# Bias and scores of two batches by 64x64 blocks of the matrix engine in an attention, Fourier and feed-forward kernel

## The chip, the core and the metric

The kernel runs on one core of a Trainium2 chip. A core has five engines with instruction streams of their own, which meet only through semaphores: the matrix engine (TensorE, PE in the profile; its weight loads are PEld), the vector engine (VectorE, DVE), the scalar engine (ScalarE, ACT), GpSimd (POOL) and SyncE (SP), which here issues most of the DMAs. PE reads SBUF and writes PSUM; ACT and DVE bring results back. The metric is the device time of one execution in microseconds.

## The reference

Four batches, 8 heads, 768 positions, 64 numbers per head. Attention with 8 global keys and a local window of 96, with a bias that falls linearly with distance; its output, 768 x 512 per batch, goes through a real-valued two-dimensional Fourier transform, a residual, a normalisation and a feed-forward layer of 512 to 2048 to 512.

```python
scores = scale * np.matmul(q, k.transpose(0, 1, 3, 2))
rel = pos[:, None] - pos[None, :]
keep = (pos[None, :] < n_global) | ((rel >= 0) & (rel < n_local))
dist = np.where(is_global & ~is_local, float(n_local), np.abs(rel))
bias = -slopes[:, None, None] * dist[None, :, :]
scores = np.where(keep, scores + bias[None], -1e9)
a = softmax(scores)
x = np.matmul(a, v)                       # (batch, 768, 512) after the heads are joined
u = x + np.real(np.fft.fft(np.fft.fft(x, axis=1), axis=2))
un = (u - mean(u)) / np.sqrt(var(u) + 1e-6)
out = u + np.maximum(un @ w_ch1, 0.0) @ w_ch2
```

## The kernel before

**Units and stages.** A unit is one pair of heads of one batch: n = 4 b + hp, 16 in all. For each unit q and k are loaded as float32 (`load`, L350), cast to half precision (`cast_qk` L405, `cast_direct` L423; the profile's tile `qk`), and transposed so that the 64 numbers of a head lie on partitions (`trans`, L556: 12 transposes on PE into `pt`, evacuated into `qkT` by DVE at L574 or ACT at L578; in batches 2 and 3 by DMA, `trans_dma`). In `qkT` the first head of the pair lies on partitions 0 to 63, the second on 64 to 127.

**Scores.** `score` (L585) works on one unit in three groups g = 0, 1, 2, each with two tiles of 128 keys against up to 256 queries (496, 480 and 384 columns per head in all). A group has a PSUM pair of banks `sc`, one bank for each head s. In batches 0 and 1 (`pem`) PE adds the bias too: for each head it multiplies a 128x128 diagonal matrix `sid`, holding minus 8 times the head's slope, with the table of distances `dist` (L600, L605), and then adds the scores, whose 64-row operands for the two heads stand in the upper and lower half of the array (L616). ACT takes the exponential straight into `ex` (L639). In batches 2 and 3 PE makes the scores alone (L614), ACT takes their exponential into `er`, and DVE multiplies by `mk` (L651), the exponential of the biased distances, which ACT makes once from `dist` (L1371, queued behind batch 1's attention).

**After the scores.** `v` is cast by POOL (L444) and, in batches 0 and 1, put in place by PE (`v_place`, 64x64 blocks of the identity, L460, tile `pvp`; evacuated by DVE L478 and ACT L479). The global keys go apart: POOL picks them out of `qkT` into `kG` (L532), then `glob` and `v_global`. `av` (L724) multiplies and DVE normalises (L769, L770) into `x`. The batch is written to DRAM and read back in another row order (`bounce`: L789 writes `xd`, L797 reads `xr`). Then the transform: DVE folds (`fold_s`, `fold_d`, L817 to L928), PE makes `py` (L954), its mirror is copied by POOL (L1002), PE makes `pu` (L1034), DVE adds the residual (L1053, L1062), and the normalised `un` is transposed: `nt_unit`, on PE into `ptu` (L1123, evacuated by ACT L1131 or DVE L1133) for pairs c below 7, by a DMA transpose from SP (`nt_dma`, L1108) for the later ones. The feed-forward layer follows for 12 pairs of rows c: `ph` (L1151, eight groups of 16 matmuls per pair), the relu of ACT or DVE (L1157, L1158), `pg` (L1175), the last sum on DVE (L1184) and the store (L1189). For pairs from 8 on a variant takes the place of `pg` (L1256 and around).

**Buffers.** The two weight matrices (loaded by POOL, L1407 and L1412, in eight blocks) lie where q and k of batch 1 were staged, so their load stands behind the last cast of q and k of unit 7. The first loads of batch 2 stand behind the last weight block (`hold`, L1421). `hT` has three buffers; one of them holds `x` of batch 1 first. `sc`, `pt`, `pvp`, `pav`, `py` and `pu` share four pairs of PSUM banks until the first `ph`, two pairs after that, and `ph` and `pg` have two banks each.

**The order.** All of it is issued in an order that a planner makes while the kernel is built (`Plan`): it keeps a clock for each engine and DMA stream, takes PE's work from four lists (mix, attention, `ph`, `pg`) and everything else from a list of pending pieces with the durations written in the code, and always issues the piece that can start first; `rank` breaks ties. A piece of rank below 0 is taken as if it were 0.8 us earlier (`AHEAD`); `RF` gives this rank to the fold of batch 0. The durations in the code have a part in the order only.

Of the kernel before, what the change touches and what calls it, by code (L numbers as in the profile page):

```python
# [9 lines left out]
FP16 = mybir.dt.float16  # L10
# [12 lines left out]
class Plan:  # L23
# [62 lines left out]
    def first(self):  # L86

        best = None
        for i, (ready, p) in enumerate(self.ready):
            if p[11]:  # L90
                ready = [max(r, self.lanes[p[11] - 1]) for r in ready]
            c = (min(max(self.t[w[0]], r) for w, r in zip(p[1], ready)) - self.AHEAD * (p[10] < 0), p[10], ready[0], p[0], i)
            if best is None or c < best:
                best = c
        return best
# [44 lines left out]
    LOOK = 10  # L140
    AHEAD = 0.8

    def run(self, streams):

        left = [list(s) for s, _ in streams]
        while True:
            best = None
            for i, s in enumerate(left):
                for k, (needs, ring, _) in enumerate(s[:self.LOOK if streams[i][1] else 1]):
                    if not self.known(needs):  # L150
                        continue
                    r = self.at(needs, "PE")
                    if ring is not None:

                        there = [(min(self.rings[g])[0], g) for g in ring
                                 if self.rings[g] and not (g in ("C", "D") and ("CD",) in self.tok)]
                        if not there:
                            continue
                        t, g = min(there)
                        r = max(r, t + self.SEM)  # L160
                    else:
                        g = None
                    c = (max(r, self.t["PE"]), i, k, g or "")
                    if best is None or c < best:
                        best = c
# [3 lines left out]
            elif best is not None:  # L169
                needs, ring, fn = left[best[1]].pop(best[2])  # L170
                fn(best[0], self.slot(best[3]) if ring is not None else "")
                self.promote()
# [28 lines left out]
def kernel(  # L201
# [40 lines left out]
    dist = np.concatenate([np.where(band, rel, np.where(kk < NG, NL, far)), near, near[:, 0:P]], 1)  # L242
    NM = 256 + 256 + P
    pp = np.arange(P)[:, None]
    mm = np.arange(P)[None, :]
# [73 lines left out]
    idn = ident[:, 0:128]  # L319
    dist_sb = kon.tile([P, NM], FP16, tag="dist", name="dist")  # L320
    sid = kon.tile([P, H, P], FP16, tag="sid", name="sid")
# [28 lines left out]
    def load(b, hp, which):  # L350
# [3 lines left out]
        if b >= FB:  # L354
            srcs = [(0, q), (1, k)] if which == "qk" else [(2, v)]
            for w, src in srcs:
                i = 1 + HP + 3 * (n - FB * HP) + w

                def run(src=src, i=i, w=w):
# [5 lines left out]
                    for t2 in range(2):  # L365
                        nc.sync.dma_start(t[64 * t2:64 * t2 + 64], x[t2])
                pl.later([("SP", 0.55 if w < 2 else 1.1, run)], free("qs", i) + gate, 0.0, [("ld", n, w)], lat=1.7, dma=1.65 if w < 2 else 2.7, nd=1 + (w > 1))
                if w < 2:
# [79 lines left out]
    def v_place(b, hp):  # L448
        n = HP * b + hp

        def run(start, ring):
# [11 lines left out]
            if n == 0:  # L463
                idle(14)
            e = pl.pe(mm_us(P, 12), start)
            pl.used(("free", "v0", n), e)
# [71 lines left out]
    def trans_dma(b, hp):  # L538
# [11 lines left out]
        for x, (w, a) in enumerate(((0, 0), (1, 0), (1, 1))):  # L550
            pl.later([("SP", 1.3, lambda w=w, a=a: xb(w, a))], [("qk", n, w)] + (free("qkT", n) if x == 0 else [("xb", n, x - 1)]), 0.0,
                     [("xb", n, x)], lat=1.7, dma=1.35 if x == 0 else 0.7)
        pl.later([("SP", 0.0, lambda: None)], [("xb", n, x) for x in range(3)], 0.0, [("qkT", n)], [("free", "qk", n)])
# [31 lines left out]
    def score(b, hp, g):  # L585
# [3 lines left out]
        def run(start, ring):  # L589
# [6 lines left out]
            if pem:  # L596
                for s in range(2):
                    lhsT = sid[:, 2 * hp + s, :]
                    if g == 1:
                        nc.tensor.matmul(pa[:, s, :].rearrange("p (i c) -> p i c", i=2)[:, :, 0:CO], lhsT,  # L600
                                         dist_sb[:, 256:256 + CO].unsqueeze(1).to_broadcast([P, 2, CO]),
                                         start=True, stop=False, skip_group_check=True)
                    else:
                        m0 = (0, 0, 256)[g]
                        nc.tensor.matmul(pa[:, s, 0:w0 + w1_], lhsT, dist_sb[:, m0:m0 + w0 + w1_],  # L605
                                         start=True, stop=False, skip_group_check=True)
            for i, c0, cw in tiles:
                for s in range(2):
                    lo = 64 * s
                    if b >= FB:  # L610
# [4 lines left out]
                        continue  # L615
                    nc.tensor.matmul(pa[:, s, c0:c0 + cw], TT[n][lo:lo + 64, 1, i * P:(i + 1) * P],  # L616
                                     TT[n][lo:lo + 64, 0, i * P:i * P + cw], start=not pem, stop=True,
                                     skip_group_check=pem)
            e = pl.pe(0.66 if pem else 0.24, start, not pem)
            pl.used(("free", "qkT", n), e)  # L620
# [178 lines left out]

    def RF(b):  # L800
        return 1 if b else -1

    def fold_s(b):
# [3 lines left out]
        for n, (c0, cw) in enumerate(parts):  # L807
# [25 lines left out]
            def f4(c0=c0, cw=cw, cell=cell):  # L833
# [6 lines left out]
                     + (free("zy", 2 * b) if n == 0 else []), 0.0,  # L840
                     [("f1", b, n)], [("free",) + XT[b]] * (2 if len(hps) == HP else 1), rank=RF(b))
            pl.later([("DVE", 2 * dve2(2 * cw), f2)], [("f1", b, n)] + free("ww", IW(b, n)), 0.0, [("f2", b, n)], rank=RF(b))
            pl.later([("DVE", 4 * dve2(cw), f3)], [("f2", b, n)], 0.0, [("f3", b, n)], rank=RF(b))
            pl.later([("DVE", 2 * dve(cw), f4)], [("f3", b, n)], 0.0, [("z", b, n)],
                     [("free", "eA", IA(b, n)), ("free", "ww", IW(b, n))], rank=RF(b))
        return [("z", b, n) for n in range(len(parts))]
# [56 lines left out]
    def fold_d(b, needs):  # L903
# [17 lines left out]
        def g2():  # L921
# [9 lines left out]
            for r, o in ((2, 12), (1, 13)):  # L931
                W[(b, r, 1)] = (ww[:, o], ww[:, o + 2])
                W[(b, r, 3)] = (ww[:, o + 4], ww[:, o + 6])
        pl.later([("DVE", 0.95 + 1.0, g1)], needs + free("eA", ia) + free("ww", IW(b, NA(b))), 0.0, [("w", b, 0)], rank=RF(b))
        pl.later([("DVE", 0.95 + 1.15, g2)], [("w", b, 0)], 0.0, [("w", b, 1)], [("free", "zy", 2 * b)], rank=RF(b))

# [168 lines left out]
    def nt_dma(c):  # L1105
        def xb():
            UNT[c] = buf("unT", c, [P, 2, ND, P], FP16, 1)
            nc.sync.dma_start_transpose(UNT[c].rearrange("p a d m -> p (a d) m"), T[("un", c)].rearrange("p a f -> p (a f)"))  # L1108
        pl.later([("SP", 1.3, xb)], [("un", c, 0), ("un", c, 1)] + free("unT", c), 0.0, [("unT", c)], [("free", "un", c)],
                 lat=1.7, dma=1.76)  # L1110

    def nt_unit(b, pr):
        c = NP * b + pr
        if c >= 7:
            return nt_dma(c)
# [223 lines left out]
    with tc.manual_schedule():  # L1339
        load(0, 0, "qk")  # L1340
        dma_const(ident, id_d, 0.3, ("c", "id"))
        dma_const(dist_sb, dist_d, 0.4, ("c", "dist"))
        load(0, 0, "v")
# [24 lines left out]
        for hp in range(HP):  # L1368
            def m(hp=hp):
                for h in (2 * hp, 2 * hp + 1):  # L1370
                    A(mk[:, h, :], dist_sb, AF.Exp, 0.0, float(-slopes[h]))  # L1371
            pl.later([("ACT", 2 * act(NM), m)], [("c", "dist")] + ([] if (0, hp) in DM else [("ex", 0, 3, 2)] if (1, hp) in DM else [("x", 1, 3, 2)]), 0.0, [("mk", hp)], rank=3)

# [163 lines left out]
```

## Time and profile before

| | us |
|---|---|
| median of 8 runs (lowest, highest) | 268.39 (267.17, 269.61) |
| the execution that was profiled | 269.61 |
| its span, first to last instruction | 267.5 |
| busy: PE, PEld, DVE, ACT, POOL | 252.9, 179.2, 176.7, 148.8, 62.8 |
| granted clock of PE, mean | 0.997 |

The 2.1 us between the execution and its span are launch and end. Of the groups of instructions, these bear on the change (engine, line, operation, count, busy us, mean ns of one):

| | busy us | mean ns |
|---|---|---|
| bias on PE: L605 128x496 x16, 128x384 x16; L600 128x480 x16 | 4.7, 4.0, 4.6 | 374, 330, 371 |
| scores on PE, batches 0 and 1: L616 x96 | 11.5 | 266, 280, 216 by shape |
| v into place on PE, 64x64 blocks: L460 x96 | 2.9 | 223 |
| exponential on ACT: L639 x24 | 20.9 | 935 |
| mk on ACT: L1371 x8 | 5.1 | 722 |
| transposition of `un` on PE: L1123 x56 | 4.5 | 219 |

How to read it: a busy time is the union of an engine's instructions; a mean is that of one instruction from start to end, and matmuls overlap, so a mean is longer than the distance from one matmul to the next. What a piece of work costs PE is therefore read from the starts in the timeline, not from the means. A wait is put down to the engine that released it last. In the slices each digit is the busy share of a fortieth of the span (6.7 us) in tenths.

### The profile page before, as it was taken

Reading aid. Unit: us, or ns where it says so; the run is one execution under the profiler, and the core shown is the slowest. Engines: PE = TensorE matmul, PEld = TensorE weight load, DVE = VectorE, ACT = ScalarE, POOL = GpSimd, SP = SyncE. Lnnn points to the kernel's source line nnn. Section 1 sums busy time; section 2 is a strip of 40 time slices with the busy share of each in tenths; the row PEclk is TensorE's granted clock in tenths of the full one; section 3 lists DMA queues with packets and bytes.
Section 4 is the critical chain, followed back from the end, with each engine's and each line's share of the span. In section 5 each row is a group of like instructions: output and inputs, shape, how many; then the busy total and the mean of one; then the engine's idle time right before and its main releaser. Section 6 shows DMA issues by size and latency. Waiting matters only on the chain.

```text
span 267.5 us, 6159 instructions
## 1 busy us (share of the span) xinstructions
PE 252.9 (95%) x2512; PEld 179.2 (67%) x2512; DVE 176.7 (66%) x364; ACT 148.8 (56%) x248; POOL 62.8 (23%) x128
## 2 busy tenths in 40 slices
PE   8998998698999999999999999899999999999993
PEld 2544654486864876776766456669767668888882
DVE  4558897653399736681359987779999645715462
ACT  1479897776556544994590255995343264443300
POOL 1442297243012242233111404311000511100000
PEclk9999999999999999999999999999999999999998
DMA  7999979999679994997599996502062340301122
GB/s 211 289 293 305 296 126 265 217 215 214 151 120 295 253 184 114 208 193 100 134 216 203 182 291 157 96 3 39 2 170 110 76 118 2 95 27 39 42 78 78
DMA packets 75181, 41.51 MB, mean 155 GB/s; under 512 B 32402, under 2 KB 71314, under 8 KB 75154
## 3 DMA queue, kind: packets, MB, share of 16 engines
q1 hardware_dynamic: 68098, 32.22, 52.6%
q0 software_dynamic: 4224, 4.19, 9.4%
q10 hardware_dynamic: 2832, 4.72, 6.0%
q8 instruction: 19, 0.31, 0.5%
q14 instruction: 8, 0.07, 0.1%
HBM read 31.42 MB, written 9.44 MB: 153 GB/s over the span
## 4 chain that ended last, share of the span: by engine, by line
PE 68%; DMA 11%; DVE 6%; SPq 5%; POOL 4%; ACT 3%; issue 1%; POOLq 0%; ACTq 0%; DVEq 0%
PE ph L1151 28%; PE pg L1175 16%; DMA qs<-in_v_dram 8%; PE pgD L1256 5%; SPq L395 4%; PE pgA L1256 4%; PE pav L750 3%; PE py L954 3%; DMA w<-in_q_dram 3%; PE pu L1034 2%; PE sc L614 2%; POOL ww L1002 2%; PE pav L739 1%; ACT qk L399 1%; SPq L1337 1%
## 5 line engine op out<-in xcount | busy, mean ns | idle before, releaser
L1151 PE MATMUL ph<-unT,w 128*128 128x256 f16 x768 | 93.4, 273 | 0.2 <-ACT eg L715 0.2
L1151 PEld LDWEIGHTS <-w 128*128 128x128 f16 x768 | 73.0, 98 | 13.9 <-issue 3.0
L1157 ACT ACTIVATE hT<-ph 128x512 f16<-128x512 f32 x76 | 45.1, 597 | 50.5 <-PE ph L1151 49.3
L1175 PE MATMUL pg<-w,hT 128*128 128x512 f16 x256 | 60.0, 379 | 0.0
L1175 PEld LDWEIGHTS <-hT 128*128 128x128 f16 x256 | 24.3, 98 | 24.3 <-issue 0.5
L639 ACT ACTIVATE ex<-sc 128x992 f16<-128x992 f32 (+2 forms) x24 | 20.9, 935 | 6.9 <-PE sc L616 6.9
L636 ACT ACTIVATE er<-sc 128x992 f16<-128x992 f32 (+2 forms) x24 | 21.8, 933 | 3.0 <-PE sc L614 2.7
L1002 POOL COPY ww<-zy 128x512 f16<-128x512 f16 x16 | 10.0, 650 | 44.9 <-PE py L954 44.8
L1184 DVE SCALAR_TENSOR_TENSOR u<-pg,sm,u 128x512 f32<-128x512 f32 x16 | 11.9, 745 | 12.7 <-PE pg L1175 12.7
L1158 DVE TENSOR_SCALAR hT<-ph 128x512 f16<-128x512 f32 x20 | 13.8, 688 | 9.3 <-PE ph L1151 9.1
L651 DVE TENSOR_TENSOR ex<-er,mk 128x992 f16<-128x992 f16 (+2 forms) x24 | 15.7, 660 | 4.6 <-ACT er L636 4.5
L750 PE MATMUL pav<-v,ex 128*128 128x65 f16 x352 | 16.3, 193 | 1.2 <-ACT ex L639 1.0
L750 PEld LDWEIGHTS <-ex 128*128 128x128 f16 x352 | 15.1, 97 | 2.9 <-issue 1.6
L399 ACT ACTIVATE qk<-qs 128x768 f16<-128x768 f32 x12 | 10.1, 846 | 9.9 <-DMA xd<-x 4.5
L1093 ACT ACTIVATE un<-un 128x512 f16<-128x512 f16 x24 | 14.9, 627 | 0.6 <-PE ptu L1123 0.6
L1100 POOL TENSOR_SCALAR sm<-sm 128x2 f32<-128x2 f32 x12 | 2.3, 192 | 52.0 <-ACT un L1093 51.8
L1053 DVE SCALAR_TENSOR_TENSOR u<-pu,xr 128x512 f32<-128x512 f32 x18 | 11.7, 687 | 4.0 <-PE pu L1034 4.0
L489 POOL CAST v<-qs 128x768 f16<-128x768 f32 x8 | 6.8, 845 | 29.8 <-DMA qs<-in_v_dram 29.7
L1256 PEld LDWEIGHTS <-hT 128*128 128x128 f16 x128 | 12.5, 98 | 1.6
L770 DVE TENSOR_TENSOR x<-pav,rc 128x512 f16<-128x512 f32 (+1 forms) x21 | 12.9, 615 | 0.7
L1274 DVE SCALAR_TENSOR_TENSOR u<-pgA,sm,u 128x256 f32<-128x256 f32 (+1 forms) x12 | 6.9, 572 | 9.9 <-PE pgA L1256 9.5
L969 ACT ACTIVATE zy<-py 128x1024 f16<-128x1024 f32 (+1 forms) x10 | 8.7, 897 | 6.5 <-PE py L954 4.9
(124 smaller groups left out, 385.9 us busy)
## 6 DMA issues: line engine op xcount, KB each, us to landing
out_dram<-u SPq DMA_DIRECT2D x24, 256.0 KB, 2.2
w<-in_moe_w_ch_dram POOLq DMA_DIRECT2D x8, 512.0 KB, 17.6
qs<-in_q_dram SPq DMA_DIRECT2D x9, 384.0 KB, 4.9
qs<-in_k_dram SPq DMA_DIRECT2D x9, 384.0 KB, 5.5
qs<-in_v_dram SPq DMA_DIRECT2D x16, 192.0 KB, 4.3
xr<-xd ACTq DMA_DIRECT2D x3, 768.0 KB, 6.1
u<-in_v_dram SPq DMA_DIRECT2D x5, 384.0 KB, 6.5
w<-in_q_dram SPq DMA_DIRECT2D x4, 384.0 KB, 6.4
```

What stands on the lines that cost most here:

```text
L636: A(mine(), cut(pa), AF.Exp, 0.0, 0.125)
L639: A(cut(expst[hp][:, :, g * 512:g * 512 + (384 if g == 2 else 512)]), cut(pa), AF.Exp, 0.0, 0.125)
L651: VT(o, mine(), m, op=ALU.mult)
L750: nc.tensor.matmul(po[:, jj, hh * 65:(hh + 1) * 65], lhsT, v16[b % 2][:, i, h, 0:65], start=(jp == 0 and a == 0), stop=(a == len(ops) - 1) ...
L770: VT(X[b][:, 2 * jp:2 * jp + 2, first * Dh:(first + nh) * Dh].rearrange("p j (h d) -> p j h d", d=Dh), pv[:, :, :, 0:Dh], rc.to_broadcast( ...
L1002: nc.gpsimd.tensor_copy(rev[:, n], T[("y", b)][:, n, :, :, ::-1])
L1093: A(x, x, AF.Square, accum_out=MV[c][:, a, 2:3])
L1151: nc.tensor.matmul(ph[:, a * CH:(a + 1) * CH].rearrange("p (x m) -> p x m", x=2), W1[0][:, d, jb * P:(jb + 1) * P], UNT[c][:, :, d, :], st ...
L1157: pl.later([("ACT", act(512), lambda: A(dst, ph, AF.Relu)), ("DVE", dve(512), lambda: V.tensor_scalar_max(dst, ph, 0.0))], [], e, [("h", c ...
L1158: ("DVE", dve(512), lambda: V.tensor_scalar_max(dst, ph, 0.0))],
L1175: nc.tensor.matmul(pg, HT[c][:, jb, t * P:(t + 1) * P], W2[0][:, jb, :], start=(jb == 0), stop=(jb == NJ - 1))
L1256: nc.tensor.matmul(o, lhs(j), rhs(j), start=(first and j == 0), stop=(j == NK - 1), skip_group_check=True)
```

## The change

1. **Bias.** The distance table is stored twice over: keys 0 to 63 and keys 64 to 127 of a tile, side by side, on both partition halves (`dist` is 128 x 2 x 640 rather than 128 x 640). Each bias matmul of 128 rows and 128 columns becomes two of 64 rows and 64 columns, one for each half t of the keys; with the two heads s that makes four, on the four quarters of the array, with the diagonal blocks of `sid` of that half.
2. **Scores of batches 0 and 1.** Each score matmul with 128 keys becomes two with 64 keys, on the same four quarters.
3. **mk** is made from the two halves of the table: 16 activations on 64 partitions for 8 on 128.
4. **Transposition of `un`**: pair 6 goes by DMA as well (`c >= 6`).
5. **The planner**: the rank below 0 for the fold of batch 0 is gone (`RF`, `AHEAD = 0.0`); a table of offsets `BIAS` is read, which is empty; several durations are new (loads, DMA transposes, `v_place`, `score`). The order of all engines comes out anew. The idle matmuls at L453 and L1356 stay.

```diff
-    AHEAD = 0.8
+    BIAS = {}
+    AHEAD = 0.0
...
+    dist = np.tile(dist.reshape(2, 64, NM).transpose(1, 0, 2), (2, 1, 1))
...
-    dist_sb = kon.tile([P, NM], FP16, tag="dist", name="dist")
+    dist_sb = kon.tile([P, 2, NM], FP16, tag="dist", name="dist")
...
-                pl.later([("SP", 0.55 if w < 2 else 1.1, run)], free("qs", i) + gate, 0.0, [("ld", n, w)], lat=1.7, dma=1.65 if w < 2 else 2.7, nd=1 + (w > 1))
+                pl.later([("SP", 0.55 if w < 2 else 1.1, run)], free("qs", i) + gate, 0.0, [("ld", n, w)], lat=1.7, dma=1.5 if w < 2 else 2.5, nd=1 + (w > 1))
...
-            e = pl.pe(mm_us(P, 12), start)
+            e = pl.pe(0.22, start, True)
...
                 for s in range(2):
-                    lhsT = sid[:, 2 * hp + s, :]
-                    if g == 1:
-                        nc.tensor.matmul(pa[:, s, :].rearrange("p (i c) -> p i c", i=2)[:, :, 0:CO], lhsT,
-                                         dist_sb[:, 256:256 + CO].unsqueeze(1).to_broadcast([P, 2, CO]),
-                                         start=True, stop=False, skip_group_check=True)
-                    else:
-                        m0 = (0, 0, 256)[g]
-                        nc.tensor.matmul(pa[:, s, 0:w0 + w1_], lhsT, dist_sb[:, m0:m0 + w0 + w1_],
-                                         start=True, stop=False, skip_group_check=True)
+                    r = slice(64 * s, 64 * s + 64)
+                    for t in range(2):
+                        o = pa[64 * t:64 * t + 64, s, :]
+                        m = dist_sb[r, t, :]
+                        if g == 1:
+                            o = o.rearrange("p (i c) -> p i c", i=2)[:, :, 0:CO]
+                            m = m[:, 256:256 + CO].unsqueeze(1).to_broadcast([64, 2, CO])
+                        else:
+                            o = o[:, 0:w0 + w1_]
+                            m0 = (0, 0, 256)[g]
+                            m = m[:, m0:m0 + w0 + w1_]
+                        nc.tensor.matmul(o, sid[r, 2 * hp + s, r], m, start=True, stop=False,
+                                         skip_group_check=True, tile_position=(64 * s, 64 * t))
...
-                    nc.tensor.matmul(pa[:, s, c0:c0 + cw], TT[n][lo:lo + 64, 1, i * P:(i + 1) * P],
-                                     TT[n][lo:lo + 64, 0, i * P:i * P + cw], start=not pem, stop=True,
-                                     skip_group_check=pem)
-            e = pl.pe(0.66 if pem else 0.24, start, not pem)
+                    for t in range(2):
+                        nc.tensor.matmul(pa[64 * t:64 * t + 64, s, c0:c0 + cw],
+                                         TT[n][lo:lo + 64, 1, i * P + 64 * t:i * P + 64 * t + 64],
+                                         TT[n][lo:lo + 64, 0, i * P:i * P + cw], start=not pem, stop=True,
+                                         skip_group_check=pem, tile_position=(lo, 64 * t))
+            e = pl.pe(0.25 + 0.21 * pem, start, True)
...
-    def RF(b):
-        return 1 if b else -1
...
-        if c >= 7:
+        if c >= 6:
             return nt_dma(c)
...
-        dma_const(dist_sb, dist_d, 0.4, ("c", "dist"))
+        dma_const(dist_sb, dist_d, 0.75, ("c", "dist"))
...
-                    A(mk[:, h, :], dist_sb, AF.Exp, 0.0, float(-slopes[h]))
-            pl.later([("ACT", 2 * act(NM), m)], [("c", "dist")] + ([] if (0, hp) in DM else [("ex", 0, 3, 2)] if (1, hp) in DM else [("x", 1, 3, 2)]), 0.0, [("mk", hp)], rank=3)
+                    for t in range(2):
+                        r = slice(64 * t, 64 * t + 64)
+                        A(mk[r, h, :], dist_sb[r, t, :], AF.Exp, 0.0, float(-slopes[h]))
+            pl.later([("ACT", 4 * act(NM), m)], [("c", "dist")] + ([] if (0, hp) in DM else [("ex", 0, 3, 2)] if (1, hp) in DM else [("x", 1, 3, 2)]), 0.0, [("mk", hp)], rank=3)
```

Left out: the offset's place in the planner's comparisons, the `rank=RF(b)` arguments that go, and the new durations of the k loads and DMA transposes.

## The prediction

> **What bounds the kernel now.** I read the page's slices first, then the chain of waits, then the timeline around the places the chain named. TensorE (PE) is busy 95%, but not evenly. Times are us from the start of the span.
>
> ```profile
> PE   8998998698999999999999999899999999999993
> DMA  7999979999679994997599996502062340301122
> ```
>
> From slice 9 (about 62 us) to the last one PE is full; before that it has holes, while the DMA row stands at 9. So there are two regimes: a head in which loads, casts and evacuations decide when PE may work, and from 62 on a PE that sets the pace. A microsecond of PE work saved after 62 is a microsecond of time. Saved before, it counts only as far as something pulls the start of the full stretch forward. All that the change makes cheaper lies before: the scores of batches 0 and 1 run from 7 to 47 us. The chain shows how the head ends:
>
> ```profile
> 33.75 1.74 POOL qk L403 x2
> 35.48 0.89 POOL w L1407
> ...
> 38.57 22.36 DMA qs<-in_v_dram
> 61.06 0.83 POOL v L444
> 61.94 0.36 PE pvp L460 x12
> ```
>
> GpSimd (POOL) casts the last q and k, issues the first weight load, and then the chain sits 22 us in a load of v (the one for unit 6), beside the weights. The v of unit 7, issued at 43.70, took 22.7 us and landed at 66.4; its cast ran from 66.52, and its placement on PE came at 68.43. From there PE never waits long. **The sum is therefore made at this placement, 68.43 us.** Two-microsecond windows of the head, each with busy time of PE, PEld, DVE, ACT, POOL, then clock, DMA share, GB/s:
>
> ```profile
> 26.00:28.00 2.00, 0.73 (x16) 0.64 (x16) 1.75 (x6) 1.98 (x4) 0.86 (x1) 1.00 1.22 309
> 34.00:36.00 2.00, 2.00 (x21) 0.79 (x19) 2.00 (x5) 2.00 (x3) 2.00 (x3) 1.00 0.70 140
> 36.00:38.00 2.00, 1.90 (x20) 1.02 (x19) 1.93 (x4) 2.00 (x3) 2.00 (x4) 1.00 0.28 24
> 50.00:52.00 2.00, 0.66 (x16) 0.32 (x15) 1.73 (x5) 0.63 (x3) 0.82 (x1) 1.00 1.18 218
> ```
>
> DMA is full up to 33.5 and from 38 to 67, and nearly empty between: **a hole of some 4 us**, after the last k has landed and before xr and the weights flow.
>
> **The scores on PE.** The timeline of one unit's start:
>
> ```profile
> 12.87 0.36 PE L460 MATMUL pvp<-v,ident 64*64 64x128 f16 x12
> 13.16 0.59 PE L605 MATMUL sc<-dist,sid 128*128 128x496 f16 x2
> ...
> 14.01 0.58 PE L600 MATMUL sc<-dist,sid 128*128 128x480 f16 x2
> ...
> 14.83 0.50 PE L605 MATMUL sc<-dist,sid 128*128 128x384 f16 x2
> 15.26 0.34 PE L616 MATMUL sc<-qkT 64*128 64x256 f16 x4
> ```
>
> From group start to group start: 0.82 (14.01 to 14.83) and 0.70 (to 15.53); the first group, undisturbed at 37.59 to 38.42, 0.83. A unit costs 2.35 us, eight units 18.8. A 256-column matmul of L1151 comes every 0.109 us, 2.35 columns a ns. The bias is two matmuls one after the other, 2x496 columns = 0.42; the scores, two at once, 496 = 0.21; the rest, 0.2, goes at the changes between a 128-row and a 64-row shape. After: the bias is four 64x64 blocks, once 496 columns if all four run at once, the scores eight blocks, again 496. A unit is 2x(496+480+384)/2350 = 1.16, plus the changes on entry and exit, about 0.15: 1.3. **Saved: 1.05 a unit, 8.4 us of PE in all.**
>
> That four run at once is not shown for 480 columns. The nearest row is L460: twelve 64x64 matmuls of 128 columns in 0.29 us (12.87 to 13.16). One at a time they need 0.65, two at once 0.33, four at once 0.16 plus a change of shape. I take four. Here a rule speaks against the change: the Trainium skill, "TensorEngine Tiling (Array Packing)", Restrictions, says column tiling switches off the fast weight load, and the change makes 12 loads a group instead of 6. By the formula of "TensorE: Matmul & The Clock Gate", LDWEIGHTS (loading the stationary operand), of 64 columns in 53 ns, one after another, twelve loads are an estimated 0.64 a group, the unit 1.9, and the saving only 3.6. L460's twelve loads and matmuls together took 0.29, so the row decides. Bounds: 3.6 to 8.9.
>
> **What this does in the head.** Not 8.4. At 26 to 28 PE waits for ACT, which casts k of unit 4 (23.54 to 24.4) and q of unit 5 between and ahead of the exponentials of unit 3, so that these end at 27.6. In the changed kernel as built, POOL takes that k, and the three exponentials run behind one q cast: with scores 0.3 earlier and loads 0.5 later I get 24.2 to 26.7. Then transposition of unit 4 at about 25.5 (was 28.02), the last normalisation of batch 0 at 30.4 (was 32.11), so:
> - The bounce: xd's second half is written at 31.0 (was 32.2), and xr's read, issued at 36.71 on its landing, goes out at about 35. Then its 0.79 MB and the v loads queued behind it fill the hole: DMA starts at 36.3 rather than 38, so this stage ends about 1.7 earlier (W2's last block 68.6 to 66.9), and the v's, now ahead of the weights, land several us earlier. SP's order up to here is unchanged.
> - Against it: the distance table grows from 160 to 320 KB; at 295 GB/s that is 0.55 us on every later load (included). POOL's last k cast now stands behind kG of unit 6, which waits for ACT's evacuation (1.49 us, L578): I get the first weight issue at 36.4 instead of 35.43. As v traffic fills that time, it costs nothing until it passes about 39; after that it costs one for one.
> - The evacuations of units 5 and 7 move from ACT (1.49 each) to DVE (0.96 each, L574), which holds fold up by one of them.
> - PE: so fold and y start only 0.7 earlier, u by 1, and the first ph at 50 (was 53.57), because the wait for v of unit 4 (1.50 at 49.85) goes. From 50, PE has the same list of work as before up to the last placement, 14.9 us, less 1.0 of waits, the weight blocks landing in time: 64.8.
>
> What is late next is PE itself. **Gain at the placement: 68.4 - 64.8 = 3.6 us**; ends: -0.5 (v no earlier, loads 0.5 later) and 6.
>
> **After 62.** (a) Transposition of unit 6 leaves PE for SP's queue (`c >= 6`). Before:
>
> ```profile
> 166.91 1.02 ACT L1131 ACTIVATE unT<-ptu 128x1024 f16<-128x1024 f16 x1 [1.17 <-PE ptu L1123]
> 167.99 1.05 PE L1034 MATMUL pu<-t,ww 128*128 128x128 f16 x16 [1.11 <-ACT unT L1131]
> ```
>
> PE saves 8 transposes (0.45) and the 1.11 wait for the bank. SP now issues a DMA transpose (1.24 us on the queue, 3.0 to landing) behind qkT's of unit 15; queued behind it are one or two of qkT's pieces, an output store and unit 7's transpose. Its reader is ph of unit 6; ahead of that PE has 16 pg matmuls (3.5 us) and scores, which cover 3.5. Gain 1.5; without cover 0. (b) mk: eight ACT instructions of 0.64 each (from 78.65, 5.12 together) become sixteen on 64 partitions. Same columns, so the same duration: +5.1 us of ACT at 75 to 87. Cover: up to the first ph of unit 2 PE runs pg, evacuated by DVE; but twelve of the sixteen stand ahead of that ph's relu, and ph has two banks. I reckon the relu at 82.7 and the third ph wanted at 83: no cost taken; up to 1.5 if the cover fails. (c) The planner's removed ranks and changed costs alter only order; the remaining waits of PE from 62 to 250 (0.49 for POOL, 0.30 and 0.16 for DVE and ACT) may go or grow by as much: 0.
>
> **Sum.** 3.6 + 1.5 = 5.1. The profiled execution took 269.61, 2.1 around its span of 267.5: it becomes 264.5. The median shown, 268.39, is 1.2 below that execution; same step: **263.3 us**. What this kernel's measurement can tell from no change is 0.5%, 1.3 us.
>
> **The rivals.**
> 1. *All of the relief counts*: PE really paces the head (slices at 9 speak for it). 8.4 + 1.5 gives 258.5; with the waits on ACT left in, 259.5. Against: PE's idle 2.9 us at 24.9 to 28 waits for ACT. 10%.
> 2. *The transfers hide it*: v7 lands where it did, plus 0.55 for the table and some of the later weight issue; placement 0 to 0.5 later, only (a) left, minus 1: 267.4. For it: DMA is at 1.2 from 38 to 67 whatever PE does. Against: the hole, and xr's place ahead of the weights. 20%.
> 3. *Slower: the clock.* The Trainium skill, "TensorE: Matmul & The Clock Gate", Part 1 (the HAM clock gate), has PE fall to half rate after an idle window of about 3.4 us. The change takes PE work out of a stretch already thin. Row: at 50 to 52 PE was busy 0.66 of 2 us and the clock stayed 1.00; so did it through the 2.0 idle us before 26.9. By the row nothing is lost. By the rule, a cold PE from 36 to 50 doubles about 10 us of y, u and score work, most of it in a chain: +8, 271. It decides once it eats over 5 us, that is, cold for more than half that stretch; one short fall costs about 2. 15%.
> The likeliest, about 263.3 (261.3 to 266), 55%. That blocks don't overlap at all (2 us and more a unit) L460 excludes.
>
> **Numbers.** The range reaches down to rival 1 and up past rival 2, leaving out the clock: 259.2 to 268.4. Faster by over 0.5% (below 267.05): 55 + 10 + a third of rival 2 = 0.71; within: 0.14; slower: 0.15.
>
> **What would show it.** A unit's three score groups in 1.3 us, bias instances starting in fours: else the block step is wrong. Exponentials of unit 3 ending near 26.7; xr issued near 35; v7 landed before 64 and its placement near 64.8: if that stands at 68, rival 2. No wait for L1131 near 162, ph of unit 6 not waiting for its transpose. mk near 10 us on ACT with no PE hole at 80 to 90. Clock 1.00 throughout. I am wrong if the placement moves by less than 2 us, or if PE's full stretch grows new waits on batch 2's loads, which hang on the last weight block and come only 1.7 earlier.

## The result, and the profile after

The changed kernel takes **270.5 us** (median of 21 runs, 268.33 to 274.13); the kernel before took 268.14 beside it. The ratio is 1.0078, 95% interval 1.0057 to 1.0098: **slower by 0.8%, about 2.1 us**, where 263.3 was forecast. The execution that was profiled took 269.98, its span 268.1. Single executions spread over 3.5 us in the kernel before (266.39 to 269.91) and 5.8 in the changed one, and the profiled ones are a long one of the first (269.61) and a short one of the second (269.98), so causes are read from the traces and sizes from the medians and ratios.

PE is busy 247.8 us, 5.1 less than before, and nothing came of it. The slices (PE, its granted clock, DMA):

```profile
PE   8687878789999799999999999999999999999993
PEclk9999799999999999999999999999999999999999
DMA  7999969999669973998779996602072331310222
```

The head, up to slice 8, is no shorter than it was, with more holes in PE; slice 4 (27 to 33 us) has a clock of 0.7. The block step itself came as reckoned. The timeline of the same unit as before (start, length, then engine, line and operation):

```profile
13.95 0.41 PE L612 MATMUL sc<-dist,sid 64*64 64x496 f16 x4
14.16 0.41 PE L624 MATMUL sc<-qkT 64*64 64x256 f16 x8
14.37 0.40 PE L612 MATMUL sc<-dist,sid 64*64 64x480 f16 x4
14.57 0.40 PE L624 MATMUL sc<-qkT 64*64 64x240 f16 x8
14.78 0.36 PE L612 MATMUL sc<-dist,sid 64*64 64x384 f16 x4
14.94 0.36 PE L624 MATMUL sc<-qkT 64*64 64x256 f16 x8
```

Group to group 0.42 and 0.41, a unit 1.2 us for 2.35: four blocks do run at once, and the many small weight loads cost nothing visible. (Twelve loads one after another, which the prediction estimated at 0.64, would take longer than the whole group did.)

What sets the head is now read from the chain of waits (start, length, what):

```profile
25.20 0.47 DVE eA L823
25.66 1.11 DVE eA L824
26.79 0.93 DVE ww L829
27.72 0.33 DVE ww L830
28.08 0.43 DVE vG L684
...
33.27 0.43 DVE x L779
34.20 0.55 DVE eA L824
34.75 0.88 DVE qkT L577
35.67 0.84 PE pt L571 x12
36.54 1.45 ACT qkT L581
37.99 0.59 ACT ex L648
38.58 6.51 DMA qs<-in_v_dram
```

From 22 to 36 us these are almost all DVE pieces: folds, normalisations, evacuations. PE appears in the stretch shown with one transposition, which itself waited for DVE. The chain then goes through ACT and one load, and after 45 back to DVE until the first `ph` at 54.58 (53.57 before). The sum of the prediction was made at the placement of v of unit 7; it came at 69.73, not at 64.8, and 1.3 later than before.

The second new thing lies at 79 to 93, on ACT (in the bracket, the idle time before and what ended it). Before:

```profile
78.65 5.12 ACT L1371 ACTIVATE mk<-dist 128x640 f16<-128x640 f16 x8 [1.17 <-issue]
86.40 0.84 ACT L399 ACTIVATE qk<-qs 128x768 f16<-128x768 f32 x1 [2.62 <-DMA qs<-in_k_dram]
88.81 0.60 ACT L1157 ACTIVATE hT<-ph 128x512 f16<-128x512 f32 x1 [1.56 <-PE ph L1151]
```

After:

```profile
78.90 8.95 ACT L1379 ACTIVATE mk<-dist 64x640 f16<-64x640 f16 x12 [2.56 <-issue]
87.87 1.09 ACT L1163 ACTIVATE hT<-ph 128x512 f16<-128x512 f32 x2
...
88.98 2.97 ACT L1379 ACTIVATE mk<-dist 64x640 f16<-64x640 f16 x4
91.98 1.51 ACT L975 ACTIVATE zy<-py 128x1024 f16<-128x1024 f32 x2
```

The relu of `ph` stands behind twelve pieces of mk, the evacuation of `py` behind four more, and PE waits for both:

```profile
88.52 1.91 PE L1157 MATMUL ph<-unT,w 128*128 128x256 f16 x16 [0.66 <-ACT hT L1163]
...
93.06 1.03 PE L960 MATMUL py<-t,ww 128*128 128x256 f16 x8 [0.89 <-ACT zy L975]
```

### The profile page after: what moved, and what is told of

Read it like the earlier page. It is cut to its first block, busy times and chain, and to the rows that moved or that the text cites. A ratio compares the mean times of both kernels' runs of the same rounds, so it can differ in the third digit from the quotient of the medians.

```text
span 268.1 us, 6442 instructions
## 1 busy us (share of the span) xinstructions
PE 247.8 (92%) x2648; PEld 182.0 (68%) x2648; DVE 179.5 (67%) x367; ACT 149.0 (56%) x247; POOL 66.3 (25%) x133
## 4 chain that ended last, share of the span: by engine, by line
PE 71%; DVE 9%; ACT 5%; DMA 5%; SPq 4%; issue 2%; POOL 2%; POOLq 0%; DVEq 0%; ACTq 0%
PE ph L1157 28%; PE pg L1181 20%; PE pgD L1262 5%; PE pgA L1262 4%; PE pav L759 3%; SPq L398 3%; PE py L960 3%; DMA qs<-in_q_dram 3%; DMA qs<-in_v_dram 2%; PE pu L1040 2%; PE sc L621 2%; POOL ww L1008 2%; DVE qkT L577 1%; PE pav L748 1%; DVE u L1068 1%
## 5 line engine op out<-in xcount | busy, mean ns | idle before, releaser
L1181 PE MATMUL pg<-w,hT 128*128 128x512 f16 x256 | 60.7, 379 | 0.0
L759 PEld LDWEIGHTS <-ex 128*128 128x128 f16 x352 | 16.2, 101 | 4.2 <-issue 3.6
L759 PE MATMUL pav<-v,ex 128*128 128x65 f16 x352 | 17.4, 198 | 1.8 <-DVE vG L684 1.3
L1164 DVE TENSOR_SCALAR hT<-ph 128x512 f16<-128x512 f32 x19 | 13.0, 687 | 6.6 <-PE ph L1157 6.2
L406 POOL CAST qk<-qs 128x768 f16<-128x768 f32 x10 | 8.7, 868 | 32.7 <-DMA qs<-in_k_dram 14.3
L1379 ACT ACTIVATE mk<-dist 64x640 f16<-64x640 f16 x16 | 11.8, 735 | 2.8 <-issue 2.6
L1090 ACT ACTIVATE un<-u,sm 128x512 f16<-128x512 f32 x10 | 7.1, 721 | 10.9 <-DVE sm L1063 10.8
```

Source lines behind the costliest of these rows:

```text
L759: nc.tensor.matmul(po[:, jj, hh * 65:(hh + 1) * 65], lhsT, v16[b % 2][:, i, h, 0:65], start=(jp == 0 and a == 0), stop=(a == len(ops) - 1) ...
L1164: ("DVE", dve(512), lambda: V.tensor_scalar_max(dst, ph, 0.0))],
L1181: nc.tensor.matmul(pg, HT[c][:, jb, t * P:(t + 1) * P], W2[0][:, jb, :], start=(jb == 0), stop=(jb == NJ - 1))
```

## The experiments

All times are compared with the kernel before, run on the same chip in between (medians 268.0 to 268.2). Where median and ratio disagree by a few tenths, both are given, since that is what the spread of single executions leaves.

| run | what it is | runs | median, us | ratio (95%) |
|---|---|---|---|---|
| | the changed kernel | 21 | 270.5 | 1.0078 (1.0057 to 1.0098) |
| e1 | all new instructions, order of before | 6 | 271.22 | 1.0122 (1.0079 to 1.0165) |
| e2 | new order, old instructions | 22 | 269.39 | 1.0044 (1.0024 to 1.0063) |
| e3 | changed kernel, mk in 8 | 14 | 268.66 | 1.0001 (0.9973 to 1.0029) |
| e4 | before, table loaded twice over | 22 | 268.57 | 1.0007 (0.9985 to 1.003) |
| e5 | e1 with mk in 8 | 22 | 268.19 | 1.0013 (0.999 to 1.0035) |
| e6 | before, pair 6 by DMA | 22 | 269.82 | 1.0061 (1.0037 to 1.0086) |
| e7 | e3, old rank of the fold | 22 | 267.93 | 1.0007 (0.9983 to 1.0031) |
| e8 | e3, first gap filled | 14 | 267.0 | 0.997 (0.9943 to 0.9998) |
| e9 | e8, pair 6 on PE | 22 | 268.53 | 0.9986 (0.9964 to 1.0008) |
| e10 | before, first gap filled | 22 | 267.68 | 0.9989 (0.9967 to 1.0012) |
| e11 | changed kernel, first gap filled | 18 | 270.11 | 1.0074 (1.0052 to 1.0095) |
| e12 | e7, first gap filled | 22 | 269.78 | 1.0056 (1.0033 to 1.0079) |
| e13 | e3, both gaps filled | 22 | 267.21 | 0.9962 (0.9942 to 0.9981) |
| e14 | changed kernel, both gaps filled | 20 | 269.24 | 1.0065 (1.0041 to 1.0089) |
| e15 | e13, pair 6 on PE | 22 | 267.47 | 0.9965 (0.9947 to 0.9984) |
| e16 | e5, both gaps filled | 6 | 270.74 | 1.0104 (1.0065 to 1.0142) |
| e17 | e13 with the old instructions | 14 | 268.24 | 1.0006 (0.9982 to 1.0029) |
| e18 | e13, half of the table made on the chip | 22 | 266.69 | 0.995 (0.9931 to 0.9969) |

### Instructions and order apart, and mk alone

The planner works on the numbers in the code, not on the instructions, so the two can be separated: e1 has the new instructions with the old numbers (every engine's order as before), e2 the old instructions with the new numbers and pair 6 by DMA.

> All the new instructions (four blocks, table twice over, mk in 16 halves), issued in the order of before (old planner durations and ranks, transposition of pair 6 on PE). Theory A, the new order loses the time: PE relief in the head pays little, the dearer table takes 1.2 us in the head at most and mk about 1.2 at 88 to 92, so 268 to 269.5, ratio to before 1.000 to 1.005, and below the changed kernel (270.5). Theory B, the blocks themselves lose it (the thinner PE lets the clock fall): 270 or more, ratio 1.007 or more, and a granted clock below 0.9 in the slice of 27 to 33 us. Theory C, table and mk lose it: 270 to 270.5 with the clock at 1.

> The changed kernel's order on every engine and pair 6 by DMA, but bias and scores by 128-wide matmuls, the table once, mk in 8 activations. Theory A (order): 270.5 or more, since PE's 1.1 us a unit comes back on top of the order: 270 to 273, ratio 1.007 to 1.018. Theory B (blocks, clock): near before, 267 to 268.5, clock 1. Theory C (table and mk): 266.5 to 268, since the gain of pair 6 stays.

e1 is slower than the changed kernel, e2 less slow. So the new order is not the main loss, and the new instructions lose even in the old order. Theory A falls in its first form. e1 fits theory B: its time is above 270, and in its profile the clock falls to 0.50 from 28.2 to 31.6 us. e2 fits none of the three. The next runs have to separate mk from the clock; e3 takes one of the new instructions out. The halves of the table are swapped on the upper 64 partitions, so that the first half is again the full table on 128 partitions:

```diff
-    dist = np.tile(dist.reshape(2, 64, NM).transpose(1, 0, 2), (2, 1, 1))
+    dist = np.concatenate([dist, np.roll(dist, 64, 0)], 1).reshape(P, 2, NM)
...
-                        m = dist_sb[r, t, :]
+                        m = dist_sb[r, (t + s) % 2, :]
...
-                    for t in range(2):
-                        r = slice(64 * t, 64 * t + 64)
-                        A(mk[r, h, :], dist_sb[r, t, :], AF.Exp, 0.0, float(-slopes[h]))
+                    A(mk[:, h, :], dist_sb[:, 0, :], AF.Exp, 0.0, float(-slopes[h]))
```

> The changed kernel, but with the halves of the table swapped on the upper 64 partitions, so that mk is again eight activations on 128 partitions; same order, same bytes. If the doubled mk costs what the idle PE at 88 to 93 shows (about 1.2 us), 269.3; if it lies beside other work, 270.5 as the changed kernel.

> The blocks and the table twice over in the order of before, with mk in eight activations (halves of the table swapped on the upper partitions); pair 6 on PE. The run with blocks in the old order and the doubled mk took 271.2. Theory A (mk is the loss, the blocks save what the head lets through): 271.2 less 2 to 2.5, 268.2 to 269.2, and if PE's relief of 8 us counts at all, below 268.2. Theory B (blocks in the old order lose by the clock or by the table): 269.5 or more.

**mk is the loss.** From the changed kernel to e3 the ratio falls by 0.0077, 2.1 us; from e1 to e5, in the old order, by 0.0109, 2.9 us; from e14 to e13, below, by 0.0103, 2.8 us (2.0 by the medians, in which nearly all runs kept the clock). ACT's timeline in e3 shows the same place:

```profile
79.06 3.87 ACT L1377 ACTIVATE mk<-dist 128x640 f16<-128x640 f16 x6 [2.59 <-issue]
85.37 1.30 ACT L1163 ACTIVATE hT<-ph 128x512 f16<-128x512 f32 x2 [2.45 <-DMA xd<-hT]
...
86.57 1.35 ACT L1377 ACTIVATE mk<-dist 128x640 f16<-128x640 f16 x2
88.58 1.51 ACT L975 ACTIVATE zy<-py 128x1024 f16<-128x1024 f32 x2 [0.65 <-DVE eA L929]
```

mk is done before the relu is wanted, ACT is idle ahead of it, and `zy` comes 3.4 earlier. PE's two waits are gone: from the start of `py` of batch 1 to its first `pu`, 7.24 us (86.74 to 93.98) for 8.84 in the changed kernel (86.61 to 95.45); in e13 and e14, which have the same order, 7.5 and 9.9; in the old order 6.1 (e5) and 8.1 (e1).

### The table

e4 is the kernel before with 320 KB of table loaded and only half of it read.

> The kernel before, only that the distance table is loaded twice over (320 KB for 160). If a dearer table delays every later load by 1.2 us and the head passes it on, 269.3, ratio 1.004; if the hole in the transfers at 34 to 38 takes it up, 268.1, ratio 1.000.

The dearer load costs 0.0007, nothing that can be told from none. In its profile the first `ph` is 0.8 later than before, but there the clock also falls, at 30 us, so the 0.8 is not the table's alone. e18 (below) asks the same from the other side.

### Pair 6

> The kernel before with one edit: the transposition of pair 6 by DMA (c >= 6), the planner going on with its old costs. My step: 1.5 us gained with cover, 266.7, ratio 0.9945. If the transfer's 3 us are not covered or another wait comes up: 268.2, ratio 1.000.

By the median not 1.5 faster but 1.6 slower in the order of before. The runs fall into two groups by their clock: five at 0.999 or more took 267.6 to 268.3, no longer than the kernel before; seventeen at 0.994 or less took 268.7 to 271.8. The profiled one (268.31, clock 1.00) is of the first group, so its waits alone are not the loss. They are, for PE from 100 to 200 us (total us, times, longest):

```profile
PE sc L614 <- DVE u L1053: 1.0, 1, 1.0
PE sc L614 <- ACT er L636: 0.6, 1, 0.6
PE sc L614 <- PE pu L1034: 0.6, 1, 0.6
PE pav L750 <- ACT er L636: 0.5, 1, 0.5
```

The wait of 1.11 for `ptu`'s bank is gone, and 2.7 us of waits of `sc` and `pav` stand in its place, since the planner sorts the next scores otherwise once the transposition is gone. They lie close together: from 165.60 to 169.01 PE is busy only 1.13 us, while in the kernel before no such stretch between 160 and 172 has less than 2.30. By the last section a stretch as thin as that can cost the clock. That it falls here in the seventeen runs is likely but not shown, as none of them was profiled.

In the new order e15 puts the pair back on PE, with the clock held:

> As e13 with pair 6 transposed on PE. In the executions of e8 and e9 with the clock held (0.996 or more) pair 6 on PE was 0.9 slower: so 267.7. My step of the prediction says 268.3 (1.5 above e13). If pair 6 is indifferent: 266.8.

0.9965 for e13's 0.9962: indifferent. e15's trace has no wait for `ptu` at all, since the next `pu` comes 1.6 us behind it and not at once; e13, in turn, waits 1.0 for ACT's `er` where e15 waits 0.5. e9 had asked it with the first gap alone filled. Its median is 1.5 above e8's, its ratio 0.4 us, but the median mixes runs with and without a fall of the clock (its profile has one at 55 us). At a clock of 0.996 or more e9 has a median of 267.6 (12 runs) and e8 266.9 (10). So with the clock held pair 6 by DMA gains between nothing (e15) and 0.7 (e9) in the new order.

> The changed kernel with mk in eight activations and the 30 idle matmuls (267.0 as measured), but the transposition of pair 6 back on PE (c >= 7). My step of 1.5 us says 268.5. If pair 6 by DMA costs as much here as it did in the order of before (1.6 us): 265.4. If it is indifferent in this order: 267.0.

### The clock

In the profile of the changed kernel the clock falls for 3.4 us, behind a stretch in which PE does little (us, busy us of PE, PEld, DVE, ACT, POOL with instructions, clock, DMA share, GB/s):

```profile
26.00:28.00 2.00, 0.74 (x6) 0.25 (x4) 1.97 (x3) 2.00 (x3) 1.22 (x2) 1.00 1.08 319
28.00:30.00 2.00, 1.45 (x26) 1.45 (x26) 1.87 (x9) 1.70 (x3) 0.00 (x0) 0.83 1.11 316
30.00:32.00 2.00, 2.00 (x32) 1.97 (x31) 1.97 (x6) 0.84 (x1) 0.37 (x2) 0.50 1.15 320
32.00:34.00 2.00, 2.00 (x34) 1.33 (x35) 1.86 (x8) 0.84 (x1) 0.00 (x0) 0.82 1.14 292
```

No single wait there is longer than 1.3 us. Of the changed kernel's 22 executions 19 show a mean clock of 0.994 or less, of 270 of the kernel before 119. To test what it costs, idle matmuls of 128 columns go where PE waits, into a part of the bank of the global scores that nobody reads: for heads 4 to 7 of batch 0 (the first gap, e8 to e12), and from e13 on for batch 1 too:

```diff
+            if (b, halves[0]) == (0, 1):
+                idle(10)
             for half in halves:
...
+            if (b, halves[0]) in ((0, 1), (1, 0)):
+                idle(20 + 4 * b)
             e = pl.pe(mm_us(512, 2 * len(halves)), start, True)
```

> The changed kernel with mk in eight activations (268.7) and 30 idle matmuls of 128 columns on the identity around the scores of the global keys of heads 4 to 7, where PE sits idle at 26 to 28.6; nothing else changed. Clock theory (the fall to 0.5 at 29 to 33 costs about 1.5 us of PE and passes it on): granted clock at 28 to 34 back to 1 and 267.5 or less. If the head is not bound by PE there: clock 1 and still 268.4 to 268.9.

> The kernel before with the same 30 idle matmuls around the global scores of heads 4 to 7. If the fall of the clock is a cost that the kernel before has too, in some of its executions: 267.4 to 267.7, ratio 0.997 to 0.999. If it is the change alone that opens the gap: 268.1, ratio 1.000.

> The changed kernel as it is, mk in sixteen activations, only with the 30 idle matmuls. If the clock's loss adds to that of mk: 268.8, ratio 1.003. If a later wait takes the gain up again: 270.5, ratio 1.008.

e8 splits by its clock: ten runs of 266.7 to 267.5 at a mean of 0.996 or more, four of 268.0 to 268.8 at 0.991 to 0.993. **Here one fall costs about 1.5 us**, and in e9 1.8 (medians of 269.4 and 267.6). It isn't a fixed price: in the kernel before, the 119 executions at 0.994 or less have a median of 268.1 and the 151 others 268.15. Why a fall costs nothing there is open. With the idle matmuls (e10) the kernel before gains 0.5 by the median, within its interval. e11 came out at its second value: the first gap is closed, but in its profile the clock falls in the next one, behind the 1.71 us in which PE waits for DVE's `un`:

```profile
52.00:54.00 2.00, 0.40 (x4) 0.24 (x5) 2.00 (x5) 1.42 (x4) 0.98 (x2) 1.00 1.21 216
54.00:56.00 2.00, 1.98 (x14) 1.58 (x15) 1.17 (x2) 1.97 (x6) 0.00 (x0) 0.73 1.23 214
56.00:58.00 2.00, 2.00 (x15) 1.64 (x14) 0.69 (x1) 0.09 (x1) 1.66 (x3) 0.50 1.25 212
```

So both gaps were filled.

> The changed kernel with mk in eight activations, 30 idle matmuls around the global scores of batch 0's heads 4 to 7, and 24 more behind the global scores of batch 1, ahead of the second gap of PE (51 to 53 us). Clock theory: clock 0.996 or more in nearly all executions, median 266.8, ratio 0.995. If other things make the spread (loads): 267 to 268.5 as before, with clocks of 0.99 still.

> The changed kernel with mk in sixteen activations, both gaps filled with idle matmuls. Clock theory: 270.5 less one fall of 1.5 to 1.7: 268.9, ratio 1.003, mk alone being left. If the clock is no cause in this kernel: 270 or more.

In e13 all 22 runs had a clock of 0.996 or more, and they lie within 2 us of each other; in e14 18 of 20 had such a clock. From e3 to e13 the ratio falls by 0.0039 (1.0 us; 1.4 by the medians), from the changed kernel to e14 by 0.0013 (0.3 us; 1.3 by the medians). The clock is a cost, then, but not the cause: with it held, the changed kernel is still slower than the kernel before (1.0065).

e7 and e12 went for the order of the fold, which stands ahead of `vG` and the normalisations in the chain above.

> The changed kernel with mk in eight activations (268.7) and the old rank of the fold of batch 0 (0.8 us of head start), the new durations kept. If the lost rank is what put the fold ahead of the normalisations and held up the head: 267 to 268, and last normalisation of batch 0 before 33. If the order's cost comes from the new durations: 268.7 or more.

> The changed kernel with mk in eight activations, the old rank of the fold of batch 0, and the 30 idle matmuls: a candidate for the fastest. If the rank's 0.7 (267.93 for 268.66) and the idle matmuls' 1.7 add: 266.3, ratio 0.993. If both mend the same delay of batch 0: 267.0 to 267.5.

e7's median is 0.7 below e3's and its ratio 0.0006 above, so the rank is not shown to matter. e12 was meant as the fastest and isn't. In its profile PE waits 1.95 us for ACT's `ex` and comes to the idle matmuls only at 27.95, when the gap they were to fill is past; they take 2.9 us, two thirds of them at half clock, and the real work behind them is late: `pvg` starts at 31.81 (27.15 in e7), the transposition of unit 4 at 33.49 (28.74), the first `ph` at 57.37 (52.96). Idle work that stands ahead of real work in PE's queue is not free.

### The price of the blocks

With mk and clock out of the way, the blocks can be priced. e17 is e13 with the instructions of before.

> Order and idle matmuls of e13 (267.21), but bias and scores by 128-wide matmuls, the table once. My step says the blocks gain 3.6: 270.8. If they are hidden in the head behind loads, casts and evacuations: 267.2, and below that by up to 1.2 if the smaller table counts. If PE paces the head after all (8 us saved in all): 272 or more.

> Blocks in the order of before, mk in eight activations, pair 6 on PE, both gaps filled. If blocks gain at a held clock what the prediction gave the head (3.6 us): 264.1. If PE's relief in the head is hidden behind loads and evacuations: 267.5 to 268, as the kernel before with idle matmuls (267.7). If the clock still falls elsewhere in this order: 268 or more with clocks of 0.99.

> As e13 (267.21), but only 160 KB of the table are loaded; ACT and POOL copy the halves across the partitions, at about 6.4 to 7.2 us. If the later loads (1.2 us) are what holds up the head: 266.0, ratio 0.992. If they are hidden: 267.2.

e17 to e13: 1.0006 to 0.9962, **the blocks gain 1.2 us** (1.0 by the medians); e2 to e3, with the clock falling, 0.0043, the same. This is net of the table, which e17 loads once and e13 twice over; to e18, which loads it once, it is 0.0056, 1.5 us. The traces say where:

| starts, us | before | after | e17 | e13 | e18 |
|---|---|---|---|---|---|
| transposition of unit 4 | 28.02 | 28.73 | 29.17 | 28.46 | 28.09 |
| first `py` | 38.46 | 40.54 | 41.12 | 39.88 | 39.50 |
| first `ph` | 53.57 | 54.58 | 54.86 | 53.94 | 53.58 |
| placement of v of unit 7 | 68.43 | 69.73 | 70.01 | 69.09 | 68.73 |

Between e17 and e13 PE's busy time from 8 to 54 us falls by 5.9 us (42.7 to 36.8; the idle matmuls are in both), and the first `ph` moves by 0.9. The rest becomes waiting: e13's longest waits of PE in the head are for DVE's `qkT`, then for ACT's `ex` and POOL's cast.

```profile
PE sc L624 <- DVE qkT L577: 1.9, 3, 0.8
PE pt L571 <- DVE qkT L577: 1.2, 1, 1.2
PE pt L571 <- ACT ex L648: 0.8, 1, 0.8
PE pt L571 <- POOL qk L406: 0.7, 2, 0.5
```

In the order of before they gain nothing that can be told: e5 (blocks, dearer table) is at 1.0013, e4 (the table alone) at 1.0007. But 18 of e5's 22 runs had lost the clock; the four others took 266.65 to 267.8. e16 missed by 3 us, with a first `ph` at 55.12 where e10, the same order with the old instructions and the first gap filled, has 52.78. In its trace PE waits 1.59 for the cast of v of unit 4 ahead of the second set of idle matmuls, not behind it, so these fill no gap: they start at 52.83 and hold up the last transposition ahead of `ph` by 1.35. It has six runs.

e18 loads 160 KB and has ACT and POOL copy the halves across (in its trace from 6.80 to 7.56 us):

```diff
-        dma_const(dist_sb, dist_d, 0.75, ("c", "dist"))
+        dma_const(dist_sb[:, 0, :], dist_d, 0.75, ("c", "dist0"))
+        pl.later([("ACT", 0.01, lambda: A(dist_sb[64:128, 1, :], dist_sb[0:64, 0, :], AF.Copy))], [("c", "dist0")], 0.0, [("c", "dist1")], rank=-1)
+        pl.later([("POOL", 0.01, lambda: nc.gpsimd.tensor_copy(dist_sb[0:64, 1, :], dist_sb[64:128, 0, :]))], [("c", "dist0"), ("c", "dist1")], 0.0, [("c", "dist")], rank=-1)
```

The head is 0.4 earlier and the median 0.5 lower; the intervals of the ratios overlap, so the half microsecond is likely, not certain. **At 266.69, ratio 0.995 (0.9931 to 0.9969), e18 is faster than both kernels**; a part of this is the idle matmuls' (e10, the kernel before with 30 of them, is at 0.9989).

## Why the prediction was wrong

**The sum.** Predicted were a gain of 3.6 in the head, 1.5 for pair 6, and 0 for mk, order and clock. Measured: blocks 1.2 gained, the dearer table included; mk 2.1 to 2.9 lost; and from e10 (old order) to e17 (new order, and pair 6 with it) 0.0017, 0.5 us lost, within the intervals. Together that is 1.4 to 2.2 lost; the changed kernel shows 2.1. That these terms cover it is no further proof: e10, e17, e13 and e14 are steps of one path, so their differences must add up. The clock adds at most 0.8 to the difference (by the medians 1.3 in the changed kernel, e14, and 0.5 in the kernel before, e10), by the ratios nothing.

**mk, the step that failed most.** "I reckon the relu at 82.7 and the third ph wanted at 83: no cost taken; up to 1.5 if the cover fails." Two terms were mis-sized. Twelve activations of 0.64 that end at 82.7 must begin at 75, which is the old start less the 3.6 expected of the head; they began at 78.90, as mk did before (78.65), behind the same issue of the write of `xd` on ACT's queue. This shift alone uncovers nothing, since the third `ph` was late as well: PE was ready for it at 87.86. But a piece on 64 partitions took 0.746 (8.95 / 12) and not 0.64, 1.3 us more over the twelve, and the relu began at 87.87: the cover of 0.3 was gone. The second half of the price wasn't looked for at all: the last four pieces stand ahead of the evacuation of `py`. PE waits 0.66 and 0.89 for the two; what else belongs to the 2.1 to 2.9 comes further on and was not traced.

**The head: right in kind, three to four times too large.** "Gain at the placement: 68.4 - 64.8 = 3.6 us." The blocks move it by 0.9 (e17 to e13), and with the new order it came 1.3 later than before, which the prediction had named as a sign of being wrong. The step that failed is the one that let scores 0.3 earlier and a cast moved to POOL pull the whole chain by 1.7 to 3.5: the exponentials of unit 3, forecast for 24.2 to 26.7, ran from 25.61 to 28.17, the last normalisation of batch 0 ended not at 30.4 but at 33.70 (32.11 before), the first weight issue not at 36.4 but at 39.88. PE was looked at as the engine that is relieved and ACT as the one it waits for; DVE, which is busy 1.75 to 2.00 of 2 in the windows that the prediction shows from 26 to 38, got one sentence, two evacuations more, of 0.96 each. It carries most of the chain from 22 to 36 and from 45 to 54 us. That DVE as a whole bounds the head is read from the chain and from PE's waits; no run relieved DVE alone.

**v and the transfers.** Here the step was right: the v of unit 7 landed at 53.9 (66.4 before) and limits nothing any more. It was no gain, because PE reaches its placement no sooner; its cast stands on POOL behind a piece of a normalisation and runs at 66.53 (66.52 before). The hole in the transfers was smaller than read: at 34 to 36 the row still has 140 GB/s. The dearer table was reckoned at 0.55 on each later load; they came 1.2 later (v of unit 0 landed at 8.8 for 7.6). By e4 that costs next to nothing, by e18 half a microsecond.

**Pair 6.** "Gain 1.5; without cover 0." With the clock held, 0 to 0.7 in the new order. The wait of 1.11 belonged to the neighbours that the old order gave the transposition, not to the transposition. In the old order the median lost 1.6, most of it in runs whose clock fell.

**The rivals.** The transfers' rival (267.4) named the right kind of outcome for the head, with the wrong engine hiding it. The clock's rival had the wrong size and the right fact: the clock falls. "By the row nothing is lost" was read from one execution, and the row of 50 to 52 kept its clock by luck of its place, as the last section shows; nor were there 2.0 idle us before 26.9, but 1.00 at a stretch and 1.7 in all from 24.9 to 28.0, where rival 1 counts 2.9. Its own "one short fall costs about 2" is near the 1.5 of e8. That its 271 lies near the 270.5 measured is luck: most of that is mk. The range, 259.2 to 268.4, left the result out because its upper end lay 1.0 above rival 2, without mk's bound of 1.5 and without the clock.

## What to carry to other kernels

A relief of one engine in a stretch where the chain runs through others is worth little: of 5.9 us of PE's work taken out of this head, where the chain names DVE, 0.9 reached its end. What a change does to a helper table (here mk, twice as many instructions on half the partitions) is part of its price at the place where the engine's queue is next wanted; ask of the queue behind it, each piece by itself. If two layouts are needed, let one of them stay what the other readers want. And where executions fall into two groups, as by the clock in e6, a profile of the one doesn't explain the median of both.

## What the runs showed of the hardware

**The clock goes by shares of a fixed window, not by idle stretches.** In the traces' record of the granted clock each fall lasts 3.41 us and begins a whole number of such windows (7, 14 or 15) after PE first ran at full clock, at 3.9 to 7.1 us. I took PE's busy time in each of these windows up to 68 us in nineteen profiles: the nine falls follow windows with 0.94 to 1.61 us of PE (after 1.61, e1 0.94, e2 1.38, e3 1.60, e4 1.49, e7 1.61, e9 1.39, e11 1.41, e12 1.46); of the other windows one had 1.59 (e12) and all the rest 1.82 or more. So about half a window of work keeps the clock. The twentieth profile, e5's, has two more falls, after 4 and 7 windows and behind 1.70 and 1.35 us; the second lasts two windows, though PE is busy 2.91 us in the first of them, so what brings the clock back is not settled here. A gap of 1.30 us lost it in the changed kernel and one of 1.71 in the same profile kept it, by where the window lies, and that differs from one execution to the next. The Trainium skill, "TensorE: Matmul & The Clock Gate", Part 1 (the HAM clock gate), speaks of an idle window of about 3.4 us that runs freely: the length and the free run agree with these traces; "idle" here means less than about half busy. The changed kernel makes the scores cheaper and so thins the window ahead of 29.3 us to 1.6; e2, the same order with the old instructions, has 2.09 or more in each of its windows there.

**An activation on half the partitions isn't cheaper, and here it was dearer.** Activations of 640 columns on 128 partitions followed one another at 0.645 us (3.87 / 6 in e3), on 64 partitions, upper and lower half in turn, at 0.746 (8.95 / 12). One alone lasts about as long, 0.722 and 0.734: on 128 partitions the next begins before the last has ended, on the halves it doesn't. Whether the number of partitions or the change of halves does this no run shows.
